# Batch 0's three-point sums moved to VectorE, and wider crossbar transfers, in an attention and Fourier-mixing kernel

## The chip, the core and the metric

The kernel runs on one core of one Trainium2 chip. A core has five engines with a queue each: TensorE (PE, matrix products; its weight loads are listed apart as PEld), VectorE (DVE), ScalarE (ACT), GpSimd (POOL) and SyncE (SP, which here only issues DMA transfers). The metric is device time in microseconds (us) of one launch; lower is better.

## The reference

Inputs are q, k, v of shape (4 batches, 8 heads, 768 positions, 64) and two MLP matrices, 512 x 2048 and 2048 x 512, all float32. Two layers follow each other.

```python
# attention: each position sees the 8 first keys and the 96 latest ones
scores = q @ k.T / sqrt(64) + bias          # bias falls with distance, per head
a = softmax(where(keep, scores, -1e9))
x = (a @ v)                                  # -> (4, 768, 512)
# Fourier mixing and MLP
mixed = real(fft(fft(x, axis=1), axis=2))    # 768 points, then 512 points
u = x + mixed
un = (u - mean(u)) / sqrt(var(u) + 1e-6)     # over the 512 columns
out = u + relu(un @ w_ch1) @ w_ch2
```

## The kernel before, in words

All products are in float16 with float32 sums. Heads are handled in pairs: batch b and pair hp give n = 4b + hp, from 0 to 15. The output of each batch is handled in three chunks of 256 rows, c = 3b + pr, from 0 to 11.

**Attention.** `load` (L327) brings q, k and v of a pair from memory; `cast_qk` and `cast_direct` round them to float16 in the tile `qk`. `trans` (L515) turns the 128 x 128 blocks: for batches 0 and 1 on TensorE, with a copy from PSUM to `qkT` (L533 VectorE, L537 ScalarE); for batches 2 and 3 by the DMA's crossbar (`trans_dma`, L499), in four transfers of 64 partitions x 768 columns for a pair. `score` (L542) makes the products of keys and queries in three groups g for each pair (`sc`, L564); in batches 0 and 1 TensorE also adds the distance bias (L554, L559), in batches 2 and 3 VectorE multiplies by the mask `mk` after ScalarE's exponential (L599). `v_place`, `v_global` and `glob` handle v and the eight global keys. `av` (L665) multiplies by v (`pav`), and VectorE divides by the sum (L710, L711), which gives `X[b]`.

**Fourier stage.** `bounce` writes `X[b]` to memory and reads it back in another order (`xr`). Along the 768 positions the transform is split into 3 x 2 parts of 128. `fold_s` (L741) is the three-point stage on VectorE: two sums and differences of halves (f1), of the second and third parts (f2), and six combinations (f3, f4). `fold_3` (L797) is the form without it: it makes the sums and differences of halves alone, and TensorE adds the three parts in the product, with an extra table `t1x` for shifted angles. `DB = 1` gives batch 0 the second form and batches 1 to 3 the first; `fold_s` is followed by `fold_d` (L841), which combines columns for the 512-point transform. `y_unit` (L878) makes the products with the tables (`py`, L892): in batch 0's form three terms where the other has one. `mirror` (L922) reverses columns on GpSimd to get the other half of a real transform (L940). `u_unit` (L961) makes the second transform (`pu`, L972), and VectorE adds `xr` (L991, L1000); mean and scale follow on ScalarE or VectorE (`un`).

**MLP.** `nt_unit` (L1052) turns `un`: chunks 0 to 6 on TensorE (`ptu`, L1063) with a copy to `unT` by ScalarE or VectorE; from chunk 7 by crossbar (`nt_dma`, L1043), two transfers of 128 x 512 columns for a chunk. `ph_unit` (L1081) is the first MLP product, eight units of eight products for a chunk (L1091); its result goes through the rectifier on ScalarE (L1097) or VectorE (L1098) into `hT`. `pg_unit` (L1104) is the second (L1114); for chunks 8 to 11 seven half-size products replace eight (`pg_units`, L1188: `pgA`, `pgD`). VectorE adds u and SP writes the result.

**What sets the order.** Nothing runs in a loop at run time. The class `Plan` works through the units when the program is built, with a cost for each and a time for each engine, and puts whichever comes first in its reckoning next in the instruction streams. `later` enters work for VectorE, ScalarE, GpSimd or SP with its needs; `pe` counts TensorE's time; `LAND` holds times before which the planner takes certain transfers as not landed. Each engine then works strictly in this order. Two banks of PSUM (tag `ph`) for the first MLP product are in the space of banks C and D, which scores, y and u of the first two batches use; so `ph_unit` needs `("CD",)`, which is there when the last of these is drained. The weights are cast while they are loaded by GpSimd's queue, into the space where q and k of batch 1 were staged; a small transfer (`hold`, L1359) makes SP wait until the last of them has landed, ahead of the first load of batch 2.

## Time and profile before

| what | us |
|---|---|
| median of 3 runs | 270.05 (268.5 to 270.39) |
| the profiled execution | 269.73 |
| its span in the trace | 268.0 |
| ScalarE busy | 151.1 (56%) |
| GpSimd busy | 60.4 (23%) |
| ph products (L1091) | 94.1, 768 of them |
| pg products (L1114) | 60.7, 256 of them |
| scores (L564), all batches | 17.0, 192 of them |
| SP's 32 transposes of q and k | 3.6 from issue to landing (median) |
| SP's 10 transposes of u | 2.4 from issue to landing (median) |

The span is what the trace covers from its first to its last instruction; the execution has 1.7 us more around it. "Busy" is the time in which at least one instruction of an engine was in work. [...] A row of the timeline gives start, length, engine, line, tiles and count, and in brackets how long the engine had been idle and what it then waited for. In the table of stages each engine's busy time stands with the number of its instructions in parentheses.

### The profile page before, as it was taken

How to read it: one execution, taken by the hardware profiler on the slowest of the kernel's cores; microseconds unless marked ns; L12 is line 12 of the kernel's file. 1: busy time of each engine (PE TensorE's matmuls, PEld its weight loads, DVE VectorE, ACT ScalarE, POOL GpSimd, SP SyncE). 2: the span in 40 equal slices, each digit the busy share in tenths (PEclk: the TensorE clock that was granted, in tenths of full speed). 3: DMA queues.
4: the chain of work that ended last, by engine and by line, in shares of the span. 5: the costliest groups of instructions: out<-in, count | busy, mean ns of one | idle time of the engine just before them, and what ended most of it. 6: DMA issues, size and time to landing. Idle time of an engine off the chain costs nothing.

```text
span 268.0 us, 6248 instructions
## 1 busy us (share of the span) xinstructions
PE 255.5 (95%) x2540; PEld 181.3 (68%) x2540; DVE 172.0 (64%) x349; ACT 151.1 (56%) x263; POOL 60.4 (23%) x127
## 2 busy tenths in 40 slices
PE   7899899989999799999999999999999999999994
PEld 2554558577855676676675356759777668888883
DVE  3666873833289575771559967778998645525473
ACT  1479693987536736995591354896443345444300
POOL 1442398142110152313110306101100511010000
PEclk9999999999999999999999999999999999999999
DMA  7999969999589985997759895402062280311122
GB/s 210 292 290 307 302 141 258 216 215 213 119 169 249 290 162 126 229 190 152 207 116 170 216 313 141 100 2 42 0 168 110 59 127 12 81 40 42 39 82 78
DMA packets 75743, 42.03 MB, mean 157 GB/s; under 512 B 32834, under 2 KB 71746, under 8 KB 75714
## 3 DMA queue, kind: packets, MB, share of 16 engines
q1 hardware_dynamic: 68658, 32.71, 50.6%
q0 software_dynamic: 4224, 4.19, 9.5%
q10 hardware_dynamic: 2832, 4.72, 7.1%
q8 instruction: 20, 0.33, 0.5%
q14 instruction: 9, 0.07, 0.1%
HBM read 31.92 MB, written 9.44 MB: 154 GB/s over the span
## 4 chain that ended last, share of the span: by engine, by line
PE 64%; DMA 20%; ACT 5%; SPq 4%; DVE 2%; POOL 2%; issue 1%; ACTq 0%; POOLq 0%
PE ph L1091 26%; PE pg L1114 12%; DMA w<-in_moe_w_ch_dram 10%; PE pgD L1195 5%; DMA qs<-in_q_dram 5%; PE py L892 4%; PE pgA L1195 4%; PE sc L564 3%; PE pu L972 3%; DMA u<-in_v_dram 3%; PE pav L691 3%; ACT ex L587 2%; DMA qs<-in_v_dram 2%; SPq L372 2%; SPq L506 2%; ACT qk L376 2%
## 5 line engine op out<-in xcount | busy, mean ns | idle before, releaser
L1091 PE MATMUL ph<-unT,w 128*128 128x256 f16 x768 | 94.1, 273 | 2.8 <-ACT hT L1097 1.7
L1091 PEld LDWEIGHTS <-w 128*128 128x128 f16 x768 | 72.7, 98 | 17.2 <-issue 6.2
L1097 ACT ACTIVATE hT<-ph 128x512 f16<-128x512 f32 x78 | 46.2, 596 | 41.7 <-PE ph L1091 41.6
L1114 PE MATMUL pg<-w,hT 128*128 128x512 f16 x256 | 60.7, 379 | 0.0
L1114 PEld LDWEIGHTS <-hT 128*128 128x128 f16 x256 | 24.1, 98 | 23.4 <-issue 0.6
L587 ACT ACTIVATE ex<-sc 128x992 f16<-128x992 f32 (+2 forms) x24 | 20.8, 924 | 8.9 <-PE sc L564 8.9
L584 ACT ACTIVATE er<-sc 128x992 f16<-128x992 f32 (+2 forms) x24 | 21.6, 924 | 5.4 <-PE sc L564 4.6
L376 ACT ACTIVATE qk<-qs 128x384 f16<-128x384 f32 (+1 forms) x29 | 13.8, 527 | 14.1 <-DMA qs<-in_q_dram 5.6
L1098 DVE TENSOR_SCALAR hT<-ph 128x512 f16<-128x512 f32 x18 | 12.4, 691 | 11.6 <-PE ph L1091 11.6
L1123 DVE SCALAR_TENSOR_TENSOR u<-pg,sm,u 128x512 f32<-128x512 f32 x16 | 12.0, 748 | 11.3 <-PE pg L1114 11.3
L466 POOL CAST v<-qs 128x768 f16<-128x768 f32 x8 | 6.6, 827 | 51.5 <-DMA qs<-in_v_dram 51.5
L564 PE MATMUL sc<-qkT 64*128 64x256 f16 (+1 forms) x192 | 17.0, 262 | 1.3 <-ACT er L584 0.6
L691 PE MATMUL pav<-v,ex 128*128 128x65 f16 x352 | 16.3, 193 | 1.0 <-DVE x L711 0.7
L599 DVE TENSOR_TENSOR ex<-er,mk 128x992 f16<-128x992 f16 (+2 forms) x24 | 14.8, 624 | 3.6 <-ACT er L584 3.5
L691 PEld LDWEIGHTS <-ex 128*128 128x128 f16 x352 | 15.2, 97 | 2.4 <-DVE x L711 0.9
L564 PEld LDWEIGHTS <-qkT 64*128 64x128 f16 x192 | 5.8, 94 | 15.5 <-issue 13.0
L1038 POOL TENSOR_SCALAR sm<-sm 128x2 f32<-128x2 f32 x12 | 2.3, 194 | 57.9 <-ACT un L1031 57.8
L907 ACT ACTIVATE zy<-py 128x1024 f16<-128x1024 f32 (+1 forms) x12 | 10.0, 846 | 9.2 <-PE py L892 8.1
L940 POOL COPY ww<-zy 128x512 f16<-128x512 f16 x16 | 9.9, 651 | 22.9 <-PE py L892 20.8
L1031 ACT ACTIVATE un<-un 128x512 f16<-128x512 f16 x24 | 14.9, 624 | 0.4 <-PE ptu L1063 0.4
L991 DVE SCALAR_TENSOR_TENSOR u<-pu,xr 128x512 f32<-128x512 f32 x18 | 11.7, 689 | 4.1 <-PE pu L972 3.2
L1195 PEld LDWEIGHTS <-hT 128*128 128x128 f16 x128 | 12.5, 98 | 1.6
(129 smaller groups left out, 381.9 us busy)
## 6 DMA issues: line engine op xcount, KB each, us to landing
out_dram<-u SPq DMA_DIRECT2D x24, 256.0 KB, 2.5
w<-in_moe_w_ch_dram POOLq DMA_DIRECT2D x8, 512.0 KB, 19.8
qs<-in_q_dram SPq DMA_DIRECT2D x9, 384.0 KB, 6.0
qs<-in_k_dram SPq DMA_DIRECT2D x9, 384.0 KB, 6.2
qs<-in_v_dram SPq DMA_DIRECT2D x16, 192.0 KB, 4.1
xr<-xd ACTq DMA_DIRECT2D x3, 768.0 KB, 5.4
u<-in_v_dram SPq DMA_DIRECT2D x5, 384.0 KB, 6.8
w<-in_q_dram SPq DMA_DIRECT2D x4, 384.0 KB, 6.6
```

The lines of the kernel that those rows point to most:

```text
L376: A(d, s, AF.Copy)
L564: nc.tensor.matmul(pa[:, s, c0:c0 + cw], TT[n][lo:lo + 64, 1, i * P:(i + 1) * P], TT[n][lo:lo + 64, 0, i * P:i * P + cw], start=(b > 1), s ...
L584: A(mine(), cut(pa), AF.Exp, 0.0, 0.125)
L587: A(cut(expst[hp][:, :, g * 512:g * 512 + (384 if g == 2 else 512)]), cut(pa), AF.Exp, 0.0, 0.125)
L599: VT(o, mine(), m, op=ALU.mult)
L691: nc.tensor.matmul(po[:, jj, hh * 65:(hh + 1) * 65], lhsT, v16[b % 2][:, i, h, 0:65], start=(jp == 0 and a == 0), stop=(a == len(ops) - 1) ...
L1031: A(x, x, AF.Square, accum_out=MV[c][:, a, 2:3])
L1091: nc.tensor.matmul(ph[:, a * CH:(a + 1) * CH], W1[0][:, d, jb * P:(jb + 1) * P], UNT[c][:, d, :], start=(d == 0), stop=(d == ND - 1))
L1097: pl.later([("ACT", act(512), lambda: A(dst, ph, AF.Relu)), ("DVE", dve(512), lambda: V.tensor_scalar_max(dst, ph, 0.0))], [], e, [("h", c ...
L1098: ("DVE", dve(512), lambda: V.tensor_scalar_max(dst, ph, 0.0))],
L1114: nc.tensor.matmul(pg, HT[c][:, jb, t * P:(t + 1) * P], W2[0][:, jb, :], start=(jb == 0), stop=(jb == NJ - 1))
L1195: nc.tensor.matmul(o, lhs(j), rhs(j), start=(first and j == 0), stop=(j == NK - 1), skip_group_check=True)
```

## The change

`DB` becomes 0: batch 0 goes through `fold_s` and `fold_d` like the others, in three column pieces of 256, 128 and 128, and the table `t1x` with its load is gone. For batches 2 and 3 a pair's transposes become two transfers of 128 partitions x 768 columns, one for q and one for k, each as soon as its own cast is done; k is loaded in two halves of 64 partitions (as v was), with even and odd positions in separate halves, and the scores and global products of these batches read q in runs of 64 elements. Chunks of u from 3 on (not 7) are turned by crossbar, a whole chunk of 128 x 1024 columns at once, and `unT` has the two halves of a chunk one behind the other. The converted v of batches 0 and 1 has a buffer of its own (`v0`) instead of a share in `er`. The planner's model changes: eight places for transfers in flight (`lanes`), 0.1 us for each switch between TensorE's tilings (`narrow`), and other values in `LAND`. So the order of the instructions changes on every engine.

```diff
-    LAND = {("xw", 0, 0): 36.0, ("xw", 0, 1): 37.6, ("xr", 0): 43.3, ("ld", 4, 2): 50.1, ("ld", 5, 2): 55.5, ("ld", 6, 2): 60.9,
...
+    LAND = {("xw", 0, 0): 34.3, ("xw", 0, 1): 36.3, ("xr", 0): 40.7, ("ld", 4, 2): 47.9, ("ld", 5, 2): 53.5, ("ld", 6, 2): 58.9, ("ld", 7, 2): 64.3, ("w1", 0): 44.8, ("w1", 1): 48.4, ("w1", 2): 52.4, ("w1", 3): 55.8, ("w2", 0): 59.5, ("w2", 1): 63.2, ("w2", 2): 66.5, ("w2", 3): 69.0}
...
+        self.lanes = [0.0] * 8
...
+            if p[11]:
+                ready = [max(r, self.lanes[p[11] - 1]) for r in ready]
...
+        for _ in range(nd):
+            self.lanes.append(max(end + lat, self.t[eng] + 2.2, *[self.LAND.get(o, 0.0) for o in outs]))
+            self.lanes.pop(0)
...
-    def pe(self, us, after=0.0):
+    narrow = False
+
+    def pe(self, us, after=0.0, narrow=False):
+        if narrow != self.narrow:
+            us += 0.1
+        self.narrow = narrow
...
-    DB = 1
+    DB = 0
+    DM = ()
...
-                    if w < 2:
+                    if w < 1:
                         run_dma(t.rearrange("p (m t) d -> p m (t d)", t=2), src, b, h0)
                         return
                     x = src[b, h0:h0 + 2].rearrange("h s d -> (h s) d").rearrange("(n m t) d -> t m n d", m=64, t=2)
                     for t2 in range(2):
                         nc.sync.dma_start(t[64 * t2:64 * t2 + 64], x[t2])
...
-            V0[n] = buf("er", n, [P, NP, 2, 2, Dh], FP16, 1)
+            V0[n] = buf("v0", n, [P, NP, 2, 2, Dh], FP16, 1)
...
-        def xb(a, t):
+        def xb(w):
             if n not in TT:
                 TT[n] = buf("qkT", n, [P, 2, S], FP16, 6)
-            o = TT[n].rearrange("p w (i a t m) -> p a t (w i) m", a=2, t=2, m=64)[:, a, t]
-            nc.sync.dma_start_transpose(o, qk16[n][64 * a:64 * a + 64, t].rearrange("p w i h d -> p (w i h d)"))
...
+            nc.sync.dma_start_transpose(TT[n][:, w].rearrange("p (j x) -> p j x", x=P),
+                                        qk16[n][:, w].rearrange("p n t h d -> p (n t h d)"))
+        for w in range(2):
+            pl.later([("SP", 1.3, lambda w=w: xb(w))], [("qk", n, w)] + (free("qkT", n) if w == 0 else [("xb", n, 0)]), 0.0,
+                     [("xb", n, w)], lat=1.9, dma=0.5)
...
+                    if b >= FB:
+                        nb = 1 if cw == P else 2
+                        o = pa[:, s, c0:c0 + nb * P]
+                        o = o.rearrange("p (y t m) -> p y t m", y=2, t=2) if nb == 2 else o.rearrange("p (t m) -> p t m", t=2)
+                        nc.tensor.matmul(o, TT[n][lo:lo + 64, 1, i * P:(i + 1) * P], tile_of(n, lo, 0, i, nb), start=True, stop=True)
+                        continue
...
-        for a in range(2):
-            def xb(a=a):
-                if a == 0:
-                    UNT[c] = buf("unT", c, [P, ND, CH], FP16, 1)
-                nc.sync.dma_start_transpose(UNT[c][:, :, a * P:(a + 1) * P], T[("un", c)][:, a])
...
+        def xb():
+            UNT[c] = buf("unT", c, [P, 2, ND, P], FP16, 1)
+            nc.sync.dma_start_transpose(UNT[c].rearrange("p a d m -> p (a d) m"), T[("un", c)].rearrange("p a f -> p (a f)"))
...
-        if c >= 7:
+        if c >= 3:
             return nt_dma(c)
...
-        def t1x_load():
-            T1X[0] = buf("hT", 3, [P, 5, 384], FP16, 4 * DB)
-            nc.sync.dma_start(T1X[0].rearrange("p a b -> p (a b)"), t1x_d.ap())
...
-                        pl.later([("SP", 0.55, t1x_load)], free("hT", 3), 0.0, [("c", "t1x")], lat=1.7, dma=1.6)
```

`tile_of`, which is new, only names the 128 queries of a block in the new layout, in runs of 64.

## The prediction

> **What bounds the kernel now.** I read the page's busy shares first, then busy time by stage, then TensorE in order of time, because a share over the whole span hides where TensorE has nothing to do.

> ```profile
> PE 255.5 (95%) x2540; PEld 181.3 (68%) x2540; DVE 172.0 (64%) x349; ACT 151.1 (56%) x263; POOL 60.4 (23%) x127
> ...
> DMA  7999969999589985997759895402062280311122
> ```

> TensorE is busy for 255.5 of 268.0 us. The DMA engines are about full for the first 60% of the span and idle at the end.

> ```profile
> core 0: us, PE busy (x) PEld busy (x) DVE busy (x) ACT busy (x) POOL busy (x), PEclk, DMA share, GB/s
> 24.00:37.90 13.90, 12.13 (x149) 6.31 (x148) 12.18 (x27) 11.59 (x14) 5.82 (x9) 1.00 0.94 271
> 37.90:44.40 6.50, 6.50 (x61) 5.82 (x62) 1.38 (x2) 3.38 (x6) 5.71 (x9) 1.00 0.89 200
> 44.40:54.30 9.90, 8.85 (x112) 5.59 (x110) 7.28 (x18) 7.83 (x17) 3.44 (x9) 1.00 1.20 215
> 54.30:76.40 22.10, 21.89 (x297) 17.89 (x297) 9.04 (x19) 15.10 (x34) 5.83 (x10) 1.00 1.02 192
> 76.40:106.20 29.80, 28.08 (x232) 19.47 (x229) 22.27 (x43) 17.37 (x32) 6.76 (x14) 1.00 0.85 193
> ```

> Columns: the stretch, its length, busy time of each engine with its instructions, clock, DMA share and rate. Between 24 and 37.9 us VectorE (12.18) and ScalarE (11.59 of 13.9) are nearly as full as TensorE. From 37.9 to 44.4 TensorE alone is full: these are the y products of batch 0, and VectorE works 1.38 of 6.5 us.

> ```profile
> 54.30 2.91 PE L1091 MATMUL ph<-unT,w 128*128 128x256 f16 x24 [1.05 <-ACT ex L587]
> 88.62 1.03 PE L1091 MATMUL ph<-unT,w 128*128 128x256 f16 x8 [1.72 <-ACT hT L1097]
> 153.81 0.34 PE L564 MATMUL sc<-qkT 64*128 64x256 f16 x4 [0.64 <-ACT er L584]
> ```

> At 54.3 us the MLP products (ph) begin; they need the early PSUM banks, so all scores of batch 1 and all of batch 0's u must be drained by then. From there to the last product TensorE stands still for only 0.21+1.72+0.64+0.18+0.38+0.18 = 3.3 us (summed from the timeline). So **two things set the time: when ph starts, and how much TensorE work lies behind that point**.

> [...]

> **The change part by part.**

> *TensorE.* Batch 0's y products fall from 60 to 24: 36 x 109 ns = 3.9 us. Chunks 3 to 6 are no longer transposed on TensorE: 4 units x 0.45 us (eight in 0.45 at 104.08) = 1.8 us. Scores of batches 2 and 3 that had 240 columns get 256: 48 x 7 ns = 0.3 us; global products of those batches are 16 of half length instead of 8: under 0.1 us. The built order has 29 runs of scores instead of 31[...]. Sum -5.4 us. Operands in 64-element runs do not appear on the moving side of any row; I cost them at nothing, because a 2x240 broadcast operand (370 ns) is no slower than a plain 496 (376). If each score took twice its 65 ns it would be +6 us.

> *VectorE.* Batch 0 gets the three-point stage. From batch 1's rows at 512 columns: 2x0.68 + 2x0.52 + 2x0.29 + 2x0.68 = 4.3 us; in three pieces 16 instructions more at some 0.06 us fixed cost each (estimate from 0.55 for 768 against 0.35 for 384 elements, less the 0.085 that neighbours overlap): 1.0. The second fold stage has four short additions (4x0.2 end to end) for one of 0.47: 0.3. Sum +5.6 us, in the stretch where VectorE has 1.3 us of gaps (25.2 to 27.7) before batch 0's fold ends at 37.8. The qkT copies of pairs 6 and 7 (0.87 each), of which one was on ScalarE and one came after the fold, now stand before its end. So the first fold stage ends near 41 us (VectorE in order: x ready 31.1, copies and pieces to 39.2, then 0.87+2x0.47), the second near 43, instead of 35.8 and 37.8. y begins 3 to 5 us later but is 3.9 us shorter.

> *What waits for it.* In the built order all scores of batch 1 but the last stand ahead of y, and the copy of pair 4's transposes stands behind batch 0's six normalisations and the first sums of a piece: the first score of batch 1 moves from 29.98 to about 32.7 us. ScalarE is out of work from 30.6 to 33.2 and then the bound: 4 pairs x 2.5 us of exponentials (0.90+0.87+0.73 end to end), one cast 0.75, four y evacuations 2.1, one eg 0.6: 46.7. The mirrors on GpSimd (four of 0.6, reversal 1.0) let the third u product start at 47.7; six u additions at 0.7 and one 0.4 on VectorE end at 51.6; ph can begin at **about 52.3, 2.0 us earlier** than 54.3. Of the 3.9 us about half is lost to waiting for VectorE and ScalarE. Bounds: -3.9 (VectorE hidden) to +0.5 ([...]0.9 for one more exponential in line).

> *Behind the start of ph:* -1.8 (transposes), +0.45 (the unit of chunk 1 now comes after it), +0.3, -0.2: **-1.2 us**.

> *SP's queue.* 16 instead of 32 transposes of q and k and 9 instead of 10 of u, at 1.2 to 1.3 us of issue each if the issue does not grow with size (64x768 and 128x512 cost 1.26 and 1.22): -21 us of SP. k in two halves: 8 x 0.75 = +6 us. A whole-chunk transpose: the 131 KB one landed in 2.4 us[...]. I take nothing, because SP is not in the way of TensorE before 164 us; if issue grows in proportion, 25 us come back and SP is where it was. The load of batch 0's extra table (480 KB, 6.6 us to landing) goes: what follows, the bounce of x and the weights, moves up 1 to 2 us. The weights must land for pg: ph and av work of 20.8 us stands ahead of its second part (16 ph 14.0, attention 5.1, others), so TensorE reaches it at 73 us; they landed at 71. Covered.

> *Waits behind ph's start.* The 1.72 us at 86.9 came from ScalarE, in whose queue eight mask exponentials and the read-back of x stood ahead of a ph evacuation; they still do, but y of batch 1 now comes after 9.5 us of pg and ph and needs 9 to 10 us of VectorE sums: 0 to 1 us of waiting. Scores of batch 2 stand about 11 us of work earlier and their global product 6 us. I put waits at 2.5 instead of 3.3: **-0.8 us**, from -3.3 (none) to +6 (next part).

> Sum: -2.0 - 1.2 - 0.8 = **-4.0 us**. The profiled execution took 269.73 (span 268.0, 1.7 around it), 0.3 under the median of 270.05; so 266 us against that median.

> **The rivals.**
> *Full gain:* VectorE's sums stay hidden and ph starts at 50.4; 3.9+1.2+1.9 (few waits) = 7: 263. For it: VectorE was idle for 5.1 us of the y stretch. Against: 24 to 37.9.
> *Gain lost early:* [...]only 1.2+0.3 remain: 268.5.
> *Slower, data of batch 2 too late:* the values of batch 2's last pair are needed at about 108 us (117.6 in the old timeline, less 3.5 and less 5.8 of work moved). From the gate at 69.3 the queue must first move 12 loads of 0.39 MB, five 0.2 MB and two 0.26 MB transposes, two stores and x both ways: 8.3 MB, of which k now in 256 B pieces (the old trace moved 246 GB/s in 80-90 us, 197 in 110-120). It decides at 8.3 MB/38 us = 217 GB/s; at 180 GB/s the last lands 8 us late, and later loads are short too: 266+8 = 274. Against: no such wait in the old trace, and SP is relieved.
> *Does not do what it says:* the built order has the 36 and 32 products fewer, so hardly.

> **The numbers.** Main case (264 to 268.5) 0.58, full gain 0.14, lost early 0.14, slower 0.12, other 0.02. A measurement tells 1%, 2.7 us. Below 267.35: 0.14 and 0.49 of the main case; within: 0.09 + 0.14 + a little; above: 0.12. Range 262.5 to 270.8.

> **What would show it.** y at 41-43 us; ScalarE nearly full from 33 to 46; ph first at 51.5-53; no transposes on TensorE after chunk 2; TensorE busy near 250. It is wrong if ph starts after 54, if SP's transposes take over 2 us of issue, or if a wait on v or qkT of batch 2 near 100-110 us exceeds 3 us.

## The result: slower by 3.7 per cent

| | before | after |
|---|---|---|
| median of 4 runs, us | 270.22 (268.5 to 272.08) | 280.32 (278.5 to 281.77) |
| the profiled execution, us | 269.73 | 281.77 |
| its span, us | 268.0 | 280.0 |
| first product of ph, us | 54.30 | 53.35 |
| TensorE's waits from there on, us | 3.3 | 12.0 |
| mean granted clock of TensorE | 1.000 | 0.976 |

The ratio is 1.037 (95% interval 1.028 to 1.046); the forecast was 266 us, faster. Here and below a ratio leaves out executions that took over 1.5 per cent more than their kernel's fastest (10 of 18 in f1_c15, 6 of 20 in b1), so it can stand lower than the median beside it.

The page of the kernel after, busy shares and the line of granted clock (a digit per 7 us, 9 is full):

```profile
PE 257.0 (92%) x2480; PEld 179.3 (64%) x2480; DVE 176.0 (63%) x372; ACT 145.9 (52%) x246; POOL 62.1 (22%) x128
...
PEclk9999799999999599999999799999999999999999
```

```profile
53.35 0.81 PE L1132 MATMUL ph<-unT,w 128*128 128x256 f16 x6 [1.52 <-DVE u L1043]
...
91.25 3.57 PE L1132 MATMUL ph<-unT,w 128*128 128x256 f16 x16 [3.92 <-ACT hT L1138]
94.61 1.91 PE L1155 MATMUL pg<-w,hT 128*128 128x512 f16 x4
...
154.75 1.63 PE L1132 MATMUL ph<-unT,w 128*128 128x256 f16 x8 [4.74 <-ACT hT L1138]
```

Twice TensorE stands still, for 3.9 and 4.7 us, until ScalarE has emptied a bank of ph; and then it is slow: 16 ph in 3.57 us where 1.91 is usual, 8 in 1.63 where 1.03 is. Busy time by stage (columns as in the prediction) has the clock:

```profile
91.25:98.00 6.75, 6.75 (x33) 4.28 (x33) 0.69 (x1) 2.94 (x5) 0.00 (x0) 0.57 1.10 273
...
147.00:154.75 7.75, 2.78 (x25) 2.34 (x24) 4.54 (x10) 2.05 (x5) 0.48 (x2) 1.00 1.10 253
154.75:161.00 6.25, 6.25 (x38) 4.42 (x38) 1.25 (x2) 5.00 (x7) 0.81 (x2) 0.73 1.04 168
```

At clocks of 0.57 and 0.73 the stretches lose, by an estimate from these rows, 6.75 x 0.43 = 2.9 and 6.25 x 0.27 = 1.7 us. So of the 12.0 us by which the span grew: -0.95 at the start of ph, +8.7 waits behind it, +4.6 clock, and -1.2 of work if that term of the forecast is right; 0.8 is left over.

**Why ScalarE is late.** ScalarE (ACT its instructions, ACTq the transfers it issues) and then SP in order of time, kernel after:

```profile
78.75 3.85 ACT L1347 ACTIVATE mk<-dist 128x640 f16<-128x640 f16 x6
88.95 0.35 ACTq L781 DMA_DIRECT2D xr<-xd  x1
89.35 1.36 ACT L1347 ACTIVATE mk<-dist 128x640 f16<-128x640 f16 x2 [6.75 <-DMA qs<-in_k_dram]
90.62 1.06 ACT L1138 ACTIVATE hT<-ph 128x512 f16<-128x512 f32 x2
```

```profile
79.29 0.37 SPq L387 DMA_DIRECT2D qs<-in_q_dram  x1
79.83 2.50 SPq L532 DMA_TRANSPOSE qkT<-qk  x1
85.59 1.30 SPq L358 DMA_DIRECT2D qs<-in_k_dram  x2
```

From 82.6 to 88.95 ScalarE does nothing: at the head of its queue is the read of x (`xr`), which by the trace waited for a load of k. That k is pair 9's, of batch 2, and the x is batch 1's: none of the one's data go into the other. In the kernel before, ScalarE and SP at the same place:

```profile
79.94 3.85 ACT L1309 ACTIVATE mk<-dist 128x640 f16<-128x640 f16 x6
85.50 0.35 ACTq L738 DMA_DIRECT2D xr<-xd  x1
85.90 0.94 ACT L376 ACTIVATE qk<-qs 128x384 f16<-128x384 f32 x2 [2.10 <-DMA qs<-in_q_dram]
```

```profile
79.35 0.37 SPq L372 DMA_DIRECT2D qs<-in_q_dram  x1
79.81 0.93 SPq L372 DMA_DIRECT2D qs<-in_k_dram  x1
```

There k's load follows q's at once, and the read goes out 3.45 us sooner. The waits in the built program say why. In it every transfer that SP or ScalarE issues is given one of eight places in turn, and waits until the place's last transfer has landed (in the trace of the changed kernel its 133 transfers report on eight semaphores, and each goes out after its semaphore's last one had landed); and a staging buffer `qs` goes to whichever tile asks when one is free. For the two transfers, in the changed kernel and in the run f1_slots below:

```
after     k of pair 9, 1st half   buffer of q of pair 9: waits for its landing and GpSimd's cast of it (85.6 us)
          read of x               place of that k half
f1_slots  k of pair 9, 1st half   buffer of k of pair 8: waits for ScalarE's cast of it (78.9 us)
          read of x               place of a half of pair 8's v, landed long before
```

The plan reckons with the second pair of rows: buffer number modulo three. SP's own waits between 78 and 93 us (us in total, times, longest) show the cost in its queue. A transpose waited for ScalarE's cast, which stands behind the stop itself; q of pair 9 waited for v of pair 8, then k for q:

```profile
SPq L532 <- ACT qk L391: 3.3, 1, 3.3
SPq L387 <- DMA qs<-in_v_dram: 3.1, 1, 3.1
SPq L358 <- DMA qs<-in_q_dram: 2.2, 1, 2.2
```

ScalarE at the second stop:

```profile
146.58 1.08 ACT L1138 ACTIVATE hT<-ph 128x512 f16<-128x512 f32 x2 [2.49 <-DMA xd<-x]
153.37 0.84 ACT L391 ACTIVATE qk<-qs 128x768 f16<-128x768 f32 x1 [5.70 <-issue]
154.12 0.58 ACT L1138 ACTIVATE hT<-ph 128x512 f16<-128x512 f32 x1
```

For 5.7 us ScalarE stands on the cast of pair 15's q, an evacuation behind it. SP issued that load at 146.68, after an output store; by the same list the store waited for the place of a write of x (3.3 us, by the trace).

### The profile page after: what moved, and what is told of

The parts are those of the page before. It is cut to its first block, busy times and chain, and to the rows that moved or that the text cites. A ratio compares the mean times of both kernels' runs of the same rounds, so it can differ in the third digit from the quotient of the medians.

```text
span 280.0 us, 6115 instructions
## 1 busy us (share of the span) xinstructions
PE 257.0 (92%) x2480; PEld 179.3 (64%) x2480; DVE 176.0 (63%) x372; ACT 145.9 (52%) x246; POOL 62.1 (22%) x128
## 4 chain that ended last, share of the span: by engine, by line
PE 60%; DMA 20%; SPq 5%; POOL 4%; issue 4%; DVE 4%; ACT 2%; ACTq 0%; POOLq 0%
PE ph L1132 22%; PE pg L1155 15%; DMA w<-in_moe_w_ch_dram 9%; PE pgD L1236 5%; PE pgA L1236 4%; DMA u<-in_v_dram 3%; DMA qkT<-qk 3%; PE pu L1015 3%; PE py L935 3%; SPq L358 2%; DMA qs<-in_q_dram 2%; PE sc L598 2%; DMA qs<-in_v_dram 2%; PE pav L734 2%; DMA qs<-in_k_dram 1%
## 5 line engine op out<-in xcount | busy, mean ns | idle before, releaser
L1132 PE MATMUL ph<-unT,w 128*128 128x256 f16 x768 | 96.1, 277 | 11.0 <-ACT hT L1138 9.2
L1132 PEld LDWEIGHTS <-w 128*128 128x128 f16 x768 | 73.9, 99 | 27.0 <-issue 14.9
L1155 PE MATMUL pg<-w,hT 128*128 128x512 f16 x256 | 61.5, 384 | 0.0
L734 PE MATMUL pav<-v,ex 128*128 128x65 f16 x352 | 17.6, 198 | 0.6 <-DVE vG L659 0.5
L391 ACT ACTIVATE qk<-qs 128x768 f16<-128x768 f32 x12 | 10.1, 840 | 15.4 <-DMA qkT<-qk 6.8
L734 PEld LDWEIGHTS <-ex 128*128 128x128 f16 x352 | 16.5, 101 | 2.2 <-issue 1.1
L1139 DVE TENSOR_SCALAR hT<-ph 128x512 f16<-128x512 f32 x17 | 11.6, 689 | 9.4 <-PE ph L1132 9.1
L952 DVE CAST zy<-py 128x512 f16<-128x512 f32 (+1 forms) x8 | 6.6, 822 | 10.9 <-PE py L935 9.0
L754 DVE TENSOR_TENSOR x<-pav,rc 128x512 f16<-128x512 f32 (+1 forms) x21 | 12.9, 615 | 0.7
L935 PE MATMUL py<-t,ww 128*128 128x256 f16 x80 | 12.0, 293 | 0.2 <-DVE ww L894 0.2
```

Source lines behind the costliest of these rows:

```text
L734: nc.tensor.matmul(po[:, jj, hh * 65:(hh + 1) * 65], lhsT, v16[b % 2][:, i, h, 0:65], start=(jp == 0 and a == 0), stop=(a == len(ops) - 1) ...
L754: VT(X[b][:, 2 * jp:2 * jp + 2, first * Dh:(first + nh) * Dh].rearrange("p j (h d) -> p j h d", d=Dh), pv[:, :, :, 0:Dh], rc.to_broadcast( ...
L935: nc.tensor.matmul(o, lhsT, rhs, start=(x == 0), stop=(x == len(ops) - 1))
L1132: nc.tensor.matmul(ph[:, a * CH:(a + 1) * CH].rearrange("p (x m) -> p x m", x=2), W1[0][:, d, jb * P:(jb + 1) * P], UNT[c][:, :, d, :], st ...
L1155: nc.tensor.matmul(pg, HT[c][:, jb, t * P:(t + 1) * P], W2[0][:, jb, :], start=(jb == 0), stop=(jb == NJ - 1))
```

## The experiments

**Theory A:** ScalarE's in-order queue stands behind late transfers, evacuations of ph stand behind those, TensorE stops, and its clock falls. **Theory B:** k in halves and the crossbar transfers load the DMA engines; the data are late whoever waits. **Theory C:** VectorE's extra sums cost it. Medians are in us, ratios against the kernel before with 95% interval. The edit of f1_slots, which binds the staging buffers, is in every run whose name starts with f1_ or ends in _slots or _slots_early.

| run | median (lowest to highest), executions | ratio |
|---|---|---|
| e1 | 277.0 (272.8 to 280.7), 4 | 1.016 (1.008 to 1.023) |
| e2 | 277.5 (273.6 to 281.9), 4 | 1.018 (1.011 to 1.024) |
| e3 | 273.3 (273.0 to 273.6), 4 | 1.013 (1.009 to 1.016) |
| b1 | 270.2 (267.5 to 273.8), 20 | 0.998 (0.996 to 1.001) |
| f1_slots | 274.6 (271.9 to 276.9), 4 | 1.014 (1.007 to 1.021) |
| a_c7 | 279.1 (278.0 to 280.7), 4 | 1.035 (1.029 to 1.042) |
| a_xb | 274.1 (272.3 to 276.8), 4 | 1.013 (1.007 to 1.019) |
| a_nolane | 279.6 (277.9 to 280.6), 4 | 1.035 (1.030 to 1.041) |
| f1_c15 | 273.7 (269.3 to 276.8), 18 | 1.004 (1.001 to 1.007) |
| f1_e1 | 273.4 (273.0 to 277.1), 4 | 1.016 (1.009 to 1.023) |
| f1_fill | 272.6 (271.8 to 276.0), 6 | 1.013 (1.007 to 1.019) |
| b_slots | 269.6 (268.6 to 273.2), 12 | 0.999 (0.997 to 1.001) |
| f1_early | 276.2 (273.1 to 277.9), 4 | 1.021 (1.015 to 1.026) |
| f1_hT | 274.9 (271.7 to 275.4), 4 | 1.017 (1.012 to 1.022) |
| f1_hT_early | 275.2 (273.4 to 277.9), 6 | 1.018 (1.014 to 1.022) |
| b1_slots | 267.9 (266.1 to 274.1), 13 | 0.993 (0.990 to 0.995) |
| a_xb_slots | 275.1 (272.0 to 276.6), 4 | 1.018 (1.011 to 1.024) |
| b1_slots_early | 266.4 (266.0 to 266.6), 4 | 0.989 (0.988 to 0.991) |

### Work taken from ScalarE's queue

```diff
-        on, eng = ("ACT", nc.scalar) if b else ("SP", nc.sync)      # e1, e3, f1_e1
+        on, eng = ("ACT", nc.gpsimd) if b else ("SP", nc.sync)
...
-            copy_on(on, qk16[n][:, w].rearrange("p n t h d -> p (n t) h d"),      # e2, e3
+            copy_on("POOL", qk16[n][:, w].rearrange("p n t h d -> p (n t) h d"),
```

> The changed kernel with one edit: the writes of x to memory and the read back (xd, xr) of batches 1 to 3 are issued by GpSimd and no longer by ScalarE; the planned order is the same. Theory A (ScalarE's in-order queue stands still behind late transfers, and the evacuations of ph behind it stop TensorE for 3.9 us at 87 to 91 us and 4.7 us at 150 to 155 us, after each of which its clock is granted at 0.57 and 0.73): the first stop goes with the read, which waited in ScalarE's queue for the place of the first half of pair 9's k; the second shrinks, because SyncE's output store waited until 146.2 us for the place of the x write and the q load of pair 15 behind it. 268 to 273 us, mean granted clock at or above 0.985, waits of TensorE on hT under 5 us (before this edit 9.2). Theory B (the data of batch 2 and 3 come later because k in halves and crossbar transfers load the DMA engines; any engine would wait for them): the wait moves to another instruction, 278 to 281 us. Theory C (VectorE's extra 5.6 us of sums cost it): no effect, 279 to 281 us.

> The changed kernel with one edit: the casts of q and k of batches 2 and 3 that the plan gives to ScalarE run on GpSimd in the same places of the order. Theory A: the stop at 150 to 155 us (ScalarE's cast of pair 15's q, which waited for its load 5.7 us with an evacuation of ph behind it) goes, with the clock loss after it, 4.7 + 1.7 us; the stop at 87 to 91 us stays, since the read of x still stands in ScalarE's queue: 272 to 276 us. Theory B (late data whoever casts it): the stop only moves to the scores or to GpSimd's v casts, 278 to 282 us.

> Both edits: the x writes and reads are issued by GpSimd and the casts of q and k of batches 2 and 3 run on GpSimd. Theory A: both stops of TensorE go, 265 to 270 us with a granted clock of 0.99 or more after 40 us. Theory B: 277 us or more. A third case: GpSimd's own queue now blocks v casts and mirrors behind the late loads; then TensorE waits on v or pu instead, 270 to 276 us.

All three have lower medians than the change and none meets theory A's figure; the ratios of e1 and e2 rest on two executions each. In e1's profile the first stop is gone, but 2.46 us of waiting for an exponential appear at 105 us, and 2.18 and 1.82 near 147 and 152. In e2's, its longest execution, the first stop is gone too, against theory A's forecast: with the casts on another engine the load of k goes out at 77.47 and the read of x at 84.64. But TensorE waits 4.23 us at 98.6 for a crossbar transfer, which fits theory B at that place. e3 is the third case of its expectation:

```profile
87.02 2.28 PE L935 MATMUL py<-t,ww 128*128 128x256 f16 x10 [2.15 <-DVE ww L894]
99.75 0.28 PE L1015 MATMUL pu<-t,rev 128*128 128x128 f16 x2 [1.60 <-POOL rev L971]
```

No wait on hT over 1 us is left, but VectorE is late with the sums for y (2.15 us), and GpSimd, now with the casts, with the mirrored columns (1.60 us). Taking work off a queue helps and makes another queue late.

### One cause at a time

b1 is the kernel before with batch 0's sums on VectorE alone (`DB = 0` and the numbers of the buffers concerned).

> The kernel before with one part of the change: batch 0's three-point sums on VectorE; crossbar form, loads, transposes on TensorE and the planner's cost model as before. Theory A (the loss lies in the loads, crossbar transfers and the order made for them, the fold is worth what was forecast or a little less): 266 to 270 us. Theory C (the fold's own order and VectorE's work cost the time): 274 us or more.

It is as fast as the kernel before: theory C falls for the fold alone, and the fold brings nothing yet (see below). f1_slots changes one line of the changed kernel; every engine's order stays word for word:

```diff
-        return wk.tile(shape, dtype, tag=tag, name=f"{tag}_{i}", bufs=NBUF[tag])
+        return wk.tile(shape, dtype, tag=f"qs{i % 3}" if tag == "qs" else tag, name=f"{tag}_{i}", bufs=1 if tag == "qs" else NBUF[tag])
```

> The changed kernel with one edit: the three staging buffers of q, k and v (qs) are bound to pair and operand in the rotation that the plan assumes, number modulo three, instead of being taken by whichever tile asks when one is free. Every engine's order of instructions stays the same; only buffers, and with them the DMA places, change. Theory A (the first stop of TensorE comes from a chain: pair 9's k takes the buffer of pair 9's q, so its load waits for that q's landing and GpSimd's cast until 85.6 us, and the read of x in ScalarE's queue waits for the place of this load until 89.0): the k load is issued near 79 to 80 us, the read near 83.5, the first stop is under 1 us and the clock stays; the second stop (150 to 155 us) has another chain and stays: 273 to 277 us. Theory B (late data through DMA traffic): still 279 to 282 us.

ScalarE of f1_slots, to be held against the rows above:

```profile
78.80 3.85 ACT L1347 ACTIVATE mk<-dist 128x640 f16<-128x640 f16 x6
83.63 0.35 ACTq L781 DMA_DIRECT2D xr<-xd  x1
84.03 1.36 ACT L1347 ACTIVATE mk<-dist 128x640 f16<-128x640 f16 x2 [1.38 <-issue]
85.30 1.07 ACT L1138 ACTIVATE hT<-ph 128x512 f16<-128x512 f32 x2
```

The k load goes out at 78.92 instead of 85.59, the read at 83.63 instead of 88.95, the evacuations at 85.30 instead of 90.62, and TensorE runs on (16 ph at 87.11 in 1.91 us). The second stop stays, 4.70 us at 147.7. As forecast by theory A: **the first stop's chain is shown**. Bytes, pieces and order were the same, so B is not the cause of this stop. The edit takes back 5.7 of the 10.1 us between the medians; no run with both the new loads and the new order has a median under f1_fill's 272.6.

```diff
-        if c >= 3:       # a_c7
+        if c >= 7:
             return nt_dma(c)
...
-        if nd is None:   # a_nolane
-            nd = int(dma > 0 and ways[0][0] in ("SP", "ACT"))
+        if True:
+            nd = 0
...
-                    if w < 1:    # a_xb; casts, transfers, scores and global products of q and k as before, too
+                    if w < 2:
                         run_dma(t.rearrange("p (m t) d -> p m (t d)", t=2), src, b, h0)
```

> The changed kernel with chunks 3 to 6 of u transposed on TensorE again (crossbar only from chunk 7, as in the kernel before). Theory A: four crossbar transfers less on SyncE, 1.8 us more on TensorE; whether the two stops come depends on where the new plan puts casts and reads in ScalarE's queue, so anything from 272 to 283 us, and the trace shows stops of 3 us or more on hT where it is long. Theory B (crossbar transfers load the DMA engines): 272 to 276 us.

> The changed kernel with the plan made without DMA places (the part of the change that lets a DMA be planned only when the one eight before it has landed is taken out; all else stays). Theory A: the plan is then further from what happens, loads and the casts behind them are planned still earlier, so ScalarE's queue is blocked at least as long: 278 to 286 us. If the places were what spoiled the order, 268 to 273 us.

> The changed kernel with the loads, casts and crossbar transfers of q and k of batches 2 and 3 as before (k as one load, four transfers of 64 rows to a pair, scores and global scores reading whole tiles). The rest of the change stays. Theory B (k in 256-byte pieces and the wide transfers make the data late): 268 to 272 us. Theory A: eight DMA places to a pair instead of seven, SyncE issues more; what counts is the order, so 270 to 280 us, and where it is under 272 the trace shows no stop of TensorE over 2 us on hT.

a_c7 and a_nolane are as slow as the change, each with a stop on hT of 4.0 us near 90 us: neither the crossbar for chunks 3 to 6 nor the planned places are needed for it. a_xb has no such stop and is 2 per cent better; its edit also gives another order, so it tells less.

### The second stop and the clock

```diff
-            copy_on(on, qk16[n][:, w].rearrange("p n t h d -> p (n t) h d"),      # f1_c15
+            copy_on("POOL" if n == 15 else on, qk16[n][:, w].rearrange("p n t h d -> p (n t) h d"),
...
+            if (c, jp) == (5, 6):      # f1_fill
+                pz = bank("pg", "fill"); [nc.tensor.matmul(pz, idn, W1[0][:, 0, 0:512], start=True, stop=True) for _ in range(16)]
             ph = bank("ph", f"ph_{c}_{jp}")
...
-                      ("ACT", act(512), lambda: A(dst, ph, AF.Relu)),      # f1_hT
+                      ("ACT", act(512), lambda: V.tensor_scalar_max(dst, ph, 0.0) if c == 5 and jp in (4, 5) else A(dst, ph, AF.Relu)),
```

> The changed kernel with the staging buffers bound as planned (as in f1_slots) and one more edit: the two casts of pair 15's q and k run on GpSimd instead of ScalarE; nothing else moves. Theory A (the second stop is ScalarE's cast of pair 15's q, waiting for its load with an evacuation of ph behind it): the 4.7 us stop on hT and the lowered clock after it (8 products of ph in 1.87 us instead of 1.03) go, 267 to 270.5 us, clock at 0.985 or more. Theory B (the data are late whoever casts them): TensorE stops at the next use instead, 273 us or more.

> f1_slots with the two evacuations of ph that stand behind ScalarE's cast of pair 15's q (chunk 5, fifth and sixth pair) given to VectorE; the casts stay on ScalarE and everything else is in its place. Theory A: TensorE is freed although the q load lands as late as in f1_slots, and GpSimd has no more work, so neither the 4.7 us stop on hT nor the 2.3 us stop on the mirrored copies of f1_c15 is there: 267 to 270 us. Theory B (late data): TensorE stops for 3 us or more at its next use, 272 us or more.

> The changed kernel with the staging buffers bound as planned, and the x writes and reads of batches 1 to 3 issued by GpSimd, which takes them out of ScalarE's queue and out of the eight DMA places of the other queues. Theory A: no first stop; the second shrinks because SyncE's output store no longer waits for the place of the x write (138.6 us in f1_slots) and the q load of pair 15 goes out earlier: 269 to 273 us. Theory B: 273 to 277 us.

f1_c15: with two casts on GpSimd the 4.7 us stop on hT is gone, and its profiled execution, the second shortest, spans 268.5 us. So ScalarE's queue decides what stops there. But the 18 executions lie between 269 and 277 us, and the profile shows a new wait, 2.31 us at 151.7 for GpSimd's mirrored columns, with slow products behind it; the mirrors stand behind a cast of v that waited 1.73 us for its load. f1_hT missed its figure. TensorE of f1_hT:

```profile
143.32 1.03 PE L1132 MATMUL ph<-unT,w 128*128 128x256 f16 x8 [1.11 <-DVE hT L1138]
146.41 1.03 PE L935 MATMUL py<-t,ww 128*128 128x256 f16 x8 [2.06 <-ACT er L620]
```

The bank of ph is free early, and TensorE stops one product later: y needs a bank that holds scores, and their exponential stands in ScalarE's queue behind the same cast. The theory had named one victim of the blocked queue; there are two. f1_e1 leaves 3.10 us of the second stop, and its 273.4 misses theory A's 269 to 273. The medians of all three runs lie in theory B's ranges: taking work out of ScalarE's queue moved or shortened the wait, and data still came late (in f1_hT ScalarE's cast waited 4.60 us for its q). **What the second stop costs as a queue, and what as late data, isn't separated.**

> f1_slots with 16 matmuls of 512 columns, whose result nobody reads, put on TensorE just ahead of the product of ph that stops for 4.7 us (chunk 5, seventh pair); they are worth about 3.4 us at full clock and nothing of the kernel's own work is changed. If the loss of clock after a stop comes from TensorE's standing idle: the stop shrinks to about 1.3 us of idleness, the products after it take 1.03 us and not 1.87, and the kernel is 1 to 2 us faster than f1_slots (272.5 to 273.5 us). If the clock falls for another cause (power, the load of the other engines): the same 1.87 us after it and 274 to 277 us.

TensorE of f1_fill:

```profile
141.53 3.62 PE L1129 MATMUL fill<-w,ident 128*128 128x512 f16 x16
146.38 1.03 PE L1134 MATMUL ph<-unT,w 128*128 128x256 f16 x8 [1.23 <-ACT hT L1140]
```

ScalarE is as late as before, but TensorE stands still for 1.23 us and its next eight products take 1.03 us, not the 1.87 of f1_slots; the median is 2.0 us lower, with ranges that overlap and ratios of 1.013 and 1.014, so a gain in time isn't shown. **The clock falls because TensorE is idle**: the products' own times show it, here and, with the gap at 27 us filled, in f1_early below. From 91.25 to 96 us the changed kernel's granted clock was 0.50, from 96 to 98 us 0.75; the 0.57 and 0.73 above are means over stretches in which it recovers. Behind six gaps of 3.9 to 4.7 us the products are slow: 16 ph took 3.57 us in the changed kernel, 3.29 in a_c7, 3.13 in e2 and 2.90 in a_nolane instead of 1.91, and 8 ph 1.63 in the changed kernel and 1.87 in f1_slots instead of 1.03. But shorter gaps did it too: behind 1.81 us in a_xb_slots 8 ph took 1.87 us, behind 2.31 in f1_c15 16 products of u took 1.91 instead of 1.06, and behind two near f1_c15's beginning 130 columns take 0.30 us instead of 0.22:

```profile
26.54 0.82 PE L734 MATMUL pav<-v,ex 128*128 128x65 f16 x12 [0.51 <-DVE vG L659]
28.73 0.22 PE L723 MATMUL pav<-vG,eg 128*128 128x130 f16 x1 [1.37 <-DVE x L754]
28.79 0.35 PE L734 MATMUL pav<-v,ex 128*128 128x65 f16 x4
28.95 0.30 PE L723 MATMUL pav<-vG,eg 128*128 128x130 f16 x1
```

A gap's length alone does not settle it: behind 2.74 us in b1, 16 ph take 1.91 us:

```profile
92.34 1.91 PE L1091 MATMUL ph<-unT,w 128*128 128x256 f16 x16 [2.74 <-ACT hT L1097]
```

> The kernel before with one edit: its three staging buffers bound in the rotation that the plan assumes; every engine's order stays. Theory A (the rotation mattered in the changed kernel only because a read in ScalarE's queue stood behind it): no stop on hT over 2 us in the kernel before either way, so 268 to 271 us, within 1 per cent. If buffers taken out of turn cost both kernels alike: 262 to 266 us.

The kernel before gains nothing from bound buffers; it has no long stop that they could take away.

### What the fold is worth

b1's trace, of one of its longer executions, has the same kind of stop, 2.74 us on hT, and in its built program k of pair 9 waits in the same way for q of pair 9 (the load of k goes out at 86.33 us, and ScalarE's cast of k, at 90.87, stands ahead of an evacuation). So the bound buffers were put into b1, and, in three runs (those with "early" in their names), matmuls that nobody reads behind batch 0's attention product near 27 us, where VectorE's first fold stands ahead of a norm that TensorE waits for:

```diff
+            if (b, first, jp) == (0, 6, 0): [nc.tensor.matmul(po[:, 1, 130:512], idn, dist_sb[:, 0:382], start=True, stop=True) for _ in range(8)]
             e = pl.pe(mm_us(65, n) + (mm_us(65 * nh, 2) if jp else 0), start)
```

> The kernel before with batch 0's sums on VectorE (b1) and the staging buffers bound as planned. In b1 TensorE stopped on hT for 2.7 us near 92 us. If that stop is of the same kind as in the changed kernel, it goes: 267 to 269 us. If not, as b1: 269 to 271 us.

> b1_slots with the 8 matmuls of 382 columns that nobody reads behind batch 0's attention product near 27 us. If the idle time there lets the clock fall in some executions: fewer executions over 268 us than in b1_slots (5 of 13), 266 to 267.5 us. If the long executions have another cause: 267.5 to 268.5 us as b1_slots.

> f1_slots with 8 matmuls of 382 columns, read by nobody, behind the product of batch 0's attention after which TensorE stands idle for 1.4 us near 27.3 us (VectorE has 1.7 us of the first fold ahead of the norm that TensorE waits for). If TensorE's clock falls near 28 us because it stands idle there: no slice under 9 before 40 us, products of 130 columns in 0.22 us and not 0.30, products of ph start at 52.7 to 53.0 us in every profile (52.8 in those without the drop, 53.4 and 54.9 in those with it), 1 to 2 us faster than f1_slots: 272 to 274 us. If the idle time is not the cause: clock and time as f1_slots, 274 to 277 us.

> Both of these edits. With both stops of TensorE on hT and the early drop of the clock gone, what is left is the forecast of the change without them: 266 to 268.5 us, 0.5 to 1.5 per cent faster than the kernel before, clock at 0.995 or more. If another loss was hidden behind the stops: 269 us or more.

Busy time by stage of b1_slots:

```profile
54.00:76.40 22.40, 22.40 (x301) 18.00 (x299) 10.01 (x21) 14.14 (x32) 6.17 (x10) 1.00 0.93 181
76.40:106.00 29.60, 29.60 (x244) 20.30 (x241) 23.48 (x44) 18.09 (x36) 8.79 (x16) 1.00 0.89 207
106.00:164.00 58.00, 58.00 (x531) 37.81 (x529) 42.28 (x84) 34.06 (x60) 12.00 (x26) 1.00 0.91 191
```

From 54 to 164 us TensorE has no gap (the column after the length is its busy time). **b1_slots_early beats both kernels**: 266.4 us, 0.989 of the kernel before, and its four executions lie within 0.6 us, where b1_slots spreads over 8. The two ran on different chips, and their ratios' intervals just touch (0.988 to 0.991, 0.990 to 0.995): the gain over the kernel before is clear, the share of the added matmuls in it less so. In f1_early the added matmuls do for the clock what was expected (products of 130 columns in 0.22 us, in f1_slots up to 0.30; ph at 52.73) and yet bring no time: 1.77 us of waiting appear at 115 us and the second stop is there. f1_hT_early misses too: 3.02 us behind an exponential at 149 us.

> a_xb (the changed kernel with q and k of batches 2 and 3 loaded, cast and transposed as before; sums on VectorE, crossbar for chunks 3 to 6 of u and the planner's places and switches stay) with the staging buffers bound as planned. If loads and crossbar transfers in the new form cost what is left between f1_slots (1.014 of the kernel before) and b1_slots (0.9925): 266 to 269 us, within 0.3 per cent of b1_slots. If the order made with places and the crossbar transfers of chunks 3 to 6 cost it: 271 to 275 us.

The form of the q and k transfers isn't what is left: a_xb_slots is 2.5 per cent above b1_slots. The longest waits in its profile, of its longest execution, are 2.22 us for ScalarE's y evacuation at 155.7 and 1.81 us for a crossbar transfer of u at 105.9. What remains between them are the planned order, the crossbar for chunks 3 to 6 and v's own buffer. **These weren't separated with bound buffers; that stays open.**

## Why the prediction was wrong, point by point

- **The step that failed** is in "Waits behind ph's start": of the masks and the read of x ahead of an evacuation it said "they still do, but y of batch 1 now comes after 9.5 us of pg and ph ...: 0 to 1 us of waiting". The place was named rightly and priced by how early TensorE would come, with the read's own start left where it was. It moved from 85.50 to 88.95 us, because what it waited for changed: the place of pair 9's q load (issued at 79.35) before, of pair 9's k load (85.59) after. This stop measured 3.9 us, not 0 to 1. The second stop, 4.7 us on pair 15's q, had no place in the forecast. In all the waits measured 12.0 us, not 2.5, and cost an estimated 4.6 more in clock, for which the forecast had no term either.
- ph's start: 52.3 forecast; 53.35 in the changed kernel, whose granted clock was 0.59 from 28 to 32 us; 52.7 to 53.2 in four profiles without that drop (f1_early, a_nolane, e1, a_xb_slots), 54.92 in f1_slots, where it lasts longest. The first score of batch 1 came at 33.2 (32.7 forecast), y at 43.4 (41 to 43). The steps hold; the term of 2.0 us was some 0.5 us too large, and the clock takes up to 2 us more.
- TensorE's work: 36 products of y and 32 transposes went and 8 global products came, as counted: 60 fewer. A product of y was put at 109 ns; in the trace before, 16 ph take 1.75 us up to the start of the product behind them. Two runs of scores fewer were put at 0.2 us, an estimate from the same trace: eight ph take 0.97 to 0.98 us up to the start of scores, 0.87 to 0.89 up to that of 128-row products. With it the terms of the sum give -5.5 us, not -5.4. The upper bound for ph's start holds 1.6 us for two delays like L829's: it took 1.58 us beside a 128x768 cast on GpSimd, L756 1.60 beside another such cast, and the other twelve 128x1536 additions and subtractions 0.94 to 0.96. Two such delays are 1.3 us. Neither moves the forecast. The 64-element runs cost nothing: four scores take 0.34 to 0.39 us, as before.
- SP's issue: a crossbar transfer of q or k takes 1.24 us of issue at the least (before 1.18) and 1.64 in the median (before 1.26), one of u 1.26 in the median (before 1.22). With twice the size it doesn't double. From issue to landing the medians are 4.7 us for q or k (before 3.6) and 3.1 for u (before 2.4). SP was nevertheless in the way, which the step had taken at nothing: not by issue but by waiting, 3.1 us for v and 2.2 for q of a buffer out of turn.
- The rival that ended slower (batch 2's data too late at under 217 GB/s) named the loads and the wrong mechanism: from 69.3 to 107 us the DMA engines moved 186 GB/s, in both kernels, and yet no wait on v or on qkT of batch 2 near 100 to 110 us reached 1 us in the changed kernel, whose first stop had also put that need off. At the first stop the load was late by buffer and place, not by bytes.
- "Gain lost early" comes true in another version: in b1_slots_early ph starts at 54.16, hardly earlier than before. The 3.2 us that it gains in span come from behind that point: 0.2 us of waits instead of 3.3.

## What to carry to other kernels

Ask of every transfer in a compute engine's queue what else it waits for than its data: the buffer and the completion place it is given, and whose transfer held them; a change elsewhere can hand it a late one, and everything behind it pays. Bind buffers to the rotation that a hand-made order assumes. Price an idle TensorE at its gap and at the slow products after it (1.66 us more for 16 of them here), and compare variants only after such accidents of order are taken out of both.

## What the runs showed that was not expected

- A gap of 3.9 us made the next 16 products cost 1.66 us more (3.57 against 1.91). Filling 3.6 us of the second stop with products that nobody reads brought the next 8 from 1.87 to 1.03 us.
- With 8 matmuls put near a gap of 1.1 us, the executions lay between 266.0 and 266.6 us (four), where without them they lay between 266.1 and 274.1 (13, on another chip). The clock isn't all of that spread: two of the 13, at 267.9 and 269.1 us, had mean clocks of 1.000 and 0.998.
- A load of k in halves landed in 4.8 us in the median where the whole took 6.2, but each half holds a place.
